# Moving the Fourier stage of a third batch into a feed-forward tail, loading normed rows a group ahead, and taking the first norms later

## The chip, the cores and the metric

The kernel runs on one core of a Trainium2 chip. The metric is the device time of one execution in microseconds (us), lower is better. The median of three executions of the kernel before is 1059.48 us. The core has a matrix engine (TensorE, PE), three engines for elementwise work (VectorE or DVE, ScalarE or ACT, GpSimd or POOL), and a queue engine (SyncE, SP) that here only issues transfers; ACT and POOL issue transfers too. Each engine works through its own list of instructions strictly in order.

## The reference, cut to what matters

Four batches of 576 rows and 512 columns (8 heads of 64 in the attention) go through three layers:

```python
x = attention(q, k, v)                 # thresholded softmax, 4 batches
k = np.maximum(xk @ w_k, 0.0)          # feed-forward block, xk and xr mix
v = k * k @ w_v                        # a row with the row before it
x = v / (1.0 + np.exp(-(xr @ w_r)))
u = x + real(fft(fft(x, axis=1), axis=2))     # Fourier stage, per batch
un = (u - mean(u)) / sqrt(var(u) + 1e-6)      # norm, per row
out = u + np.maximum(un @ w_ch1, 0.0) @ w_ch2 # channel mixer
```

Everything is float32. Products are made from high and low parts, three matmuls for one.

## The kernel before, in words

The rows of each batch are handled in two halves in the feed-forward block and in groups of 256 rows after it; there are nine groups, g = 0 to 8, two for each batch and one of remainder rows.

The **attention** fills the first half of the time, and the feed-forward blocks of the first batches run between its steps. The generator `ffn_stream` gives out the feed-forward work piece by piece: for each half a k phase (8 products `kps`), an r phase (4 products `rps`, whose gate is a tanh on ACT, L524) and a v phase (4 products `vps`, combined with the gate on DVE, L543); the rows are then transposed, copied to `xnat` by ACT (L572) and stored to DRAM (`xd[b]`, L574).

When the attention has ended, the loop `for _ in stream` (L1204) runs what is left of that generator: the v phase of the second half of batch 2, and all of batch 3. Beside each piece it advances other generators: `side`, the **Fourier stage** of batches 0 and 1, at 0.6 steps for each piece (`P['SR']`), with the norms of groups 0 and 1 between the steps of batch 1; and, from the middle of the last k phase on, `cgen`, which loads and unpacks the first quarter of the channel weights (`quarter(0)`, two pieces at a time). When the last r phase is done (`r_done`), groups 0 and 1 are transposed by `turn`.

The Fourier stage of a batch has 11 steps. `fft_fold` (6) loads the rows (`load_pairs`, and the remainder rows by `load_rem`) and folds them on DVE; `fft_one` (3) makes 35 matmuls (`f`); `fft_two` (2) makes 33 (`fz`, `fa`, `fb`), and `make_u` adds them on DVE into u and stores it (`ud[g]`, on SP).

The **channel mixer** (`mixer`, L1133) then goes through four quarters q of the weights and the nine groups in a written order that begins (0,0), (0,1), (0,2), (0,3), (1,0) to (1,3), (0,4). For each it makes `ch1` (`c1ps`, into two PSUM buffers, emptied by ACT L1119 and DVE L1120 into `hh`) and `ch2` (`c2ps`), adds the sum to `u` and stores that. Beside it the generator `behind` advances two steps for each piece: first `quarter(1)` (16 steps, each of four DVE passes over a tile `wraw` that ACT has issued a load for), then the Fourier stages of batches 2 and 3, then the remainder group and `done`, which frees the Fourier buffers. The norm of a later group is made at fixed places (`ahead_of`): group 2 in (0,0), group 3 in (0,1), and so on.

`norm(g)` loads the 256 rows of a group from `ud[g]` (two transfers, L995), takes statistics on DVE (L998), a square root on ACT (L1003), and scales the rows on ACT (L1011). Its rows live in a ring of four buffers with the tag "o", which `xnat`, the remainder rows of `load_rem` and `fft_last` use too.

The order in the source is a priority, not the final order: a planner places every instruction on its engine's list by its own estimate of when the inputs are there, and work of lower priority fills what it believes to be idle. Once placed, the order is fixed. The two lines of the source that speak of order most directly are these:

```python
    side = chain(fft_fold(0), fft_one(0), fft_two(0), fft_fold(1), norms(), fft_one(1), fft_two(1))
    ahead_of = {(0, 0): 2, (0, 1): 3, (1, 2): 4, (1, 3): 5, (0, 5): 6, (0, 6): 7, (0, 7): 8}
```

Of the kernel before, what the change touches and what calls it, by code (L numbers as in the profile page):

```python
# [10 lines left out]
F32 = mybir.dt.float32  # L11
# [9 lines left out]
D, FF, FC = 512, 1024, 2048  # L21
# [8 lines left out]
def tile_kernel(ctx: ExitStack, tc: tile.TileContext, a):  # L30
# [835 lines left out]
    def fft_fold(b):  # L866
        while written[b] < 2:
            yield
        settle()
        prs = prs_of[b] = load_pairs(b)  # L870
        ra, rb = load_rem(b)
        parts_e, parts_o = [], []
        for xa, xb in prs:
            e, o = folded(xa, xb, 128)
            yield
            parts_e.append(split_tile(e, 257, "fse"))
            parts_o.append(split_tile(o, 256, "fso"))
            yield
        e, o = folded(ra, rb, 98)
        yield  # L880
        ske = stack_tile(e, 257, "ske")
        sko = stack_tile(o, 256, "sko")
        fold_of[b] = (parts_e, parts_o, ske, sko)
        yield

    def fft_one(b):
        parts_e, parts_o, ske, sko = fold_of.pop(b)
        G = [fp.tile([128, 2, 290], F32R, tag=f"G{i}", bufs=1, name=f"G{i}") for i in range(2)]
        Hh = [fp.tile([128, 2, HS], F32R, tag=f"H{i}", bufs=1, name=f"H{i}") for i in range(2)]
        for mc in range(2):  # L890
            o = stage_1(parts_e, ske, tc1, tc1r, 290, 128 * mc, 128 * mc + 128)
            fsplit(G[0][:, mc], G[1][:, mc], o)
            o = stage_1(parts_o, sko, ts1, ts1r, HS, 128 * mc, 128 * mc + 128)
            fsplit(Hh[0][:, mc], Hh[1][:, mc], o)
            yield
        o = stage_1(parts_e, ske, tc1, tc1r, 290, 256, 257)
        fsplit(g1[0:1], g1[32:33], o)
        sl = slice(32 * b, 32 * b + 32)
        act.activation(g1[64:65, sl], o[:, 256:288], AF.Copy)
        dve.tensor_tensor(g1[96:97, sl], o[:, 256:288], g1[0:1, 256:288].bitcast(F32), op=ALU.subtract)  # L900
        for i, x in enumerate((G[0], G[1], Hh[0], Hh[1])):
            act.activation(grem[i][:, :, b, :], x[:, :, 256:288].bitcast(F32), AF.Copy)
        spec[b] = (G, Hh)
        yield

    def fft_two(b):
        G, Hh = spec.pop(b)
        prs = prs_of.pop(b)
        z, _ = stage_2(G, None, 0, 288, 289)
        zr = fp.tile([1, 257], F32, name="zr")  # L910
        act.activation(zr, z[0:1, 0:257], AF.Copy)
        for i in range(2):
            pa, pb = stage_2(G, Hh, 0, 128 * i, 128 * i + 128)
            make_u(2 * b + i, pa, pb, *prs[i], z=zr if i == 0 else None)
            yield

    def fft_last():
        xa = chp.tile([128, D], F32, tag="o", bufs=4, name="xar")
        xb = chp.tile([128, D], F32, tag="o", bufs=4, name="xbr")
        for b in range(B):  # L920
            sp.dma_start(xa[32 * b:32 * b + 32], xd[b][256:288, :])
            sp.dma_start(xb[32 * b:32 * b + 32], xd[b][544:576, :])
        gr = [x.rearrange("p c b r -> p c (b r)") for x in grem]
        pa, pb = stage_2(gr[0:2], gr[2:4], 64, 0, 128)
        make_u(8, pa, pb, xa, xb)
        yield

    def chain(*gens):
        for g in gens:
            yield from g  # L930
# [57 lines left out]

    uts, pairs, hs, more = {}, {}, {}, {}

    def norm(g):

        u = [chp.tile([128, D], F32, tag="o", bufs=4, name="un") for _ in range(2)]
        for j in range(2):
            sp.dma_start(u[j], ud[g][:, j])  # L995
        st = chp.tile([128, 32], F32, tag="lnst", bufs=1, name="lnst")
        for j in range(2):
            dve.bn_stats(st[:, 6 * j:6 * j + 6], u[j])  # L998
            dve.bn_aggr(st[:, 12 + 2 * j:14 + 2 * j], st[:, 6 * j:6 * j + 6])
        mean, var = st[:, 12:16:2], st[:, 13:16:2]  # L1000
        ve, sd, r0, t0, rstd, nb = (st[:, k:k + 2] for k in (16, 18, 20, 22, 24, 26))
        dve.tensor_scalar(ve, var, 1e-6, None, op0=ALU.add)
        act.activation(sd, ve, AF.Sqrt)  # L1003
        dve.reciprocal(r0, sd)
        dve.tensor_tensor(t0, r0, r0, op=ALU.mult)
        dve.tensor_tensor(t0, t0, ve, op=ALU.mult)
        dve.tensor_scalar(t0, t0, -0.5, 1.5, op0=ALU.mult, op1=ALU.add)
        dve.tensor_tensor(rstd, r0, t0, op=ALU.mult)
        dve.scalar_tensor_tensor(nb, mean, -1.0, rstd, op0=ALU.mult, op1=ALU.mult)
        for j in range(2):  # L1010
            act.activation(u[j], u[j], AF.Identity, scale=rstd[:, j:j + 1], bias=nb[:, j:j + 1])  # L1011
        return u
# [180 lines left out]
    fft_done, utp, ubp, hwp, xwp = False, None, None, None, None  # L1193
    normed = {}

    def norms():
        for g in range(2):
            normed[g] = norm(g)
            yield

    side = chain(fft_fold(0), fft_one(0), fft_two(0), fft_fold(1), norms(), fft_one(1), fft_two(1))
    cgen = None
    acc = 0.0
    for _ in stream:  # L1204
        for _ in range(2):
            if builds:
                builds.pop(0)()
        if len(pending) >= 2 or second:
            settle()
        acc += P['SR']  # L1210
        while acc >= 1:
            acc -= 1
            next(side, None)
        if ffn.get("r_done") and len(uts) < 2:
            g = len(uts)
            while g not in normed:
                next(side)
            turn(g, normed[g])
        if ffn.get("k_done") and cgen is None:
            cgen, pieces = quarter(0), 0  # L1220
        if cgen is not None:
            for _ in range(2):
                if pieces < 7 or ffn["k_done"] > 1:
                    next(cgen, None)
                    pieces += 1
# [7 lines left out]
    for _ in cgen:  # L1233
        pass
    behind = chain(
        quarter(1), fft_fold(2), fft_one(2), fft_two(2),
        fft_fold(3), fft_one(3), fft_two(3), fft_last(), done(),
    )

    ahead_of = {(0, 0): 2, (0, 1): 3, (1, 2): 4, (1, 3): 5, (0, 5): 6, (0, 6): 7, (0, 7): 8}  # L1240
# [1 line left out]
    for (q, gs), f in mixer():  # L1242
        g = gs[-1]
        credit += 2.0 if (q, g) < (0, 4) else 1.25 * len(gs)
        while credit >= 1:
            credit -= 1
            next(behind, None)
        if f == 2 and (q, g) in ahead_of:
            while (q, g) == (0, 5) and not fft_done:
                next(behind)  # L1250
            n = ahead_of[q, g]
            turn(n, norm(n))
        if (q, g) in ((1, 5), (2, 1)) and f == 3:
            for _ in behind:
                pass
            behind = quarter(q + 1)
        if q > 0 and g == 8 and f == 3:
            for _ in behind:
                pass
# [126 lines left out]
```

## Time and profile before

| | us |
|---|---|
| median of three executions | 1059.48 |
| lowest and highest | 1058.34, 1060.55 |
| the profiled execution, whole | 1057.07 |
| its span, first to last instruction | 1055.0 |
| PE busy within the span | 1004.3 |

The whole time of the profiled execution is 2.07 us more than its span. An engine's busy time leaves out its waits; of PE it has to be read with care, since matmuls overlap and their ends are modelled. The granted clock is the share of TensorE's full speed that the chip granted; its mean is 0.988.

### The profile page before, as it was taken

How to read it: one execution, taken by the hardware profiler on the slowest of the kernel's cores; microseconds unless marked ns; L12 is line 12 of the kernel's file. 1: busy time of each engine (PE TensorE's matmuls, PEld its weight loads, DVE VectorE, ACT ScalarE, POOL GpSimd, SP SyncE). 2: the span in 40 equal slices, each digit the busy share in tenths (PEclk: the TensorE clock that was granted, in tenths of full speed). 3: DMA queues.
4: the chain of work that ended last, by engine and by line, in shares of the span. 5: the costliest groups of instructions: out<-in, count | busy, mean ns of one | idle time of the engine just before them, and what ended most of it. 6: DMA issues, size and time to landing. Idle time of an engine off the chain costs nothing.

```text
span 1055.0 us, 18820 instructions
## 1 busy us (share of the span) xinstructions
PE 1004.3 (95%) x6807; PEld 884.6 (84%) x6807; DVE 715.9 (68%) x1880; ACT 536.6 (51%) x1211; POOL 395.8 (38%) x495
## 2 busy tenths in 40 slices
PE   5887889999999999999999988999999999999998
PEld 4565669988998888999799887898998888889997
DVE  6799988667776685865457978556537449236776
ACT  4688767675866757767265734342413113113332
POOL 1545868455574564843233101000014125112231
PEclk9899989999999999999999999999999999999999
DMA  6443331121211212100722656436325435223221
GB/s 223 149 134 86 112 108 60 48 72 38 72 60 54 66 47 72 51 24 14 209 72 88 205 186 200 157 103 226 129 89 184 130 114 179 97 99 122 101 100 61
DMA packets 45636, 114.52 MB, mean 109 GB/s; under 512 B 6319, under 2 KB 6740, under 8 KB 45544
## 3 DMA queue, kind: packets, MB, share of 16 engines
q1 hardware_dynamic: 27920, 74.47, 22.0%
q10 hardware_dynamic: 12344, 22.13, 6.8%
q0 software_dynamic: 5280, 16.72, 4.5%
q8 instruction: 54, 0.88, 0.4%
q14 instruction: 38, 0.31, 0.1%
HBM read 84.98 MB, written 28.32 MB: 107 GB/s over the span
## 4 chain that ended last, share of the span: by engine, by line
PE 73%; DVE 11%; DMA 7%; ACT 4%; issue 3%; POOL 1%; ACTq 0%; SPq 0%; DVEq 0%; POOLq 0%
PE c1ps L1109 6%; PE c1ps L1107 6%; PE c1ps L1108 6%; PE av L388 6%; PE s L227 5%; PE c2ps L1129 4%; PE c2ps L1131 4%; PE c2ps L1130 4%; PE p L1064 4%; PE t L329 4%; PE kps L408 2%; PE vps L536 2%; PE vps L537 2%; PE vps L538 2%; PE kps L409 2%
## 5 line engine op out<-in xcount | busy, mean ns | idle before, releaser
L267 DVE TENSOR_REDUCE small<-s 128x1 f32<-128x576 f32 x144 | 107.0, 752 | 48.1 <-PE s L227 36.9
L1178 POOL DMA_DIRECT2D ud<-u x54 | 29.4, 545 | 268.3 <-DVE u L1177 167.7
L290 POOL TENSOR_SCALAR e<-e,small 128x576 f32<-128x576 f32 x112 | 89.5, 806 | 89.0 <-DVE small L653 74.6
L282 DVE SCALAR_TENSOR_TENSOR e<-s,small,e 128x576 f32<-128x576 f32 x128 | 102.7, 812 | 25.4 <-ACT e L278 22.2
L278 ACT ACTIVATE e<-s,small 128x576 f32<-128x576 f32 x128 | 93.8, 744 | 29.4 <-DVE small L267 27.7
L1119 ACT ACTIVATE hh<-c1ps 128x256 fp32r<-128x256 f32 (+1 forms) x84 | 37.1, 443 | 138.4 <-PE c1ps L1109 114.7
L1120 DVE SCALAR_TENSOR_TENSOR hh<-c1ps,hh 128x256 fp32r<-128x256 f32 (+1 forms) x84 | 41.6, 497 | 86.6 <-ACT hh L1119 86.5
L329 PE MATMUL t<-ident,e 128*128 128x128 f32 x512 | 82.9, 279 | 10.2 <-ACT pt L332 4.6
L332 ACT ACTIVATE pt<-t 128x512 f32<-128x512 f32 x128 | 75.1, 599 | 22.8 <-PE t L329 21.0
L493 POOL TENSOR_TENSOR k<-relu,k 128x288 fp32r<-128x288 f32 x64 | 54.6, 855 | 68.4 <-ACT k L491 64.2
L329 PEld LDWEIGHTS t<-ident,e 128*128 128x128 f32 x512 | 61.6, 142 | 21.3 <-issue 6.5
L408 PE MATMUL kps<-xh,wk 128*128 128x288 f32 x256 | 78.2, 306 | 0.8 <-DVE fdd L851 0.3
L536 PE MATMUL vps<-k,wv 128*128 128x288 f32 x256 | 77.7, 305 | 0.4 <-ACT tg L524 0.4
L537 PE MATMUL vps<-k,wv 128*128 128x288 f32 x256 | 77.4, 303 | 0.0
L538 PE MATMUL vps<-k,wv 128*128 128x288 f32 x256 | 76.8, 301 | 0.0
L1107 PE MATMUL c1ps<-ut,cA 128*128 128x256 f32 (+1 forms) x224 | 71.2, 319 | 5.7 <-DVE hh L1120 4.0
L409 PE MATMUL kps<-xl,wk 128*128 128x288 f32 x256 | 76.3, 298 | 0.0
L410 PE MATMUL kps<-xh,wk 128*128 128x288 f32 x256 | 76.2, 298 | 0.0
L1109 PE MATMUL c1ps<-ut,cB 128*128 128x256 f32 (+1 forms) x256 | 76.0, 297 | 0.0
L1107 PE MATMUL c1ps<-ut,cB 128*128 128x256 f32 (+1 forms) x256 | 75.8, 296 | 0.0
L1108 PE MATMUL c1ps<-ut,cB 128*128 128x256 f32 (+1 forms) x256 | 75.7, 296 | 0.0
L1108 PE MATMUL c1ps<-ut,cA 128*128 128x256 f32 (+1 forms) x224 | 70.8, 316 | 0.2 <-DVE ut L1028 0.2
(273 smaller groups left out, 3117.4 us busy)
## 6 DMA issues: line engine op xcount, KB each, us to landing
u<-ud SPq DMA_DIRECT2D x36, 512.0 KB
wraw<-in_w_ch ACTq DMA_DIRECT2D x64, 256.0 KB
rawqk<-in_qk SPq DMA_DIRECT2D x24, 608.0 KB
ud<-u POOLq DMA_DIRECT2D x54, 256.0 KB, 2.6
v<-in_v SPq DMA_DIRECT2D x16, 320.0 KB
un<-ud SPq DMA_DIRECT2D x18, 256.0 KB
out<-u SPq DMA_DIRECT2D x18, 256.0 KB
wraw<-in_w_k SPq DMA_DIRECT2D x8, 512.0 KB
```

Of the source, the lines that this page charges most:

```text
L267: dve.tensor_reduce(st[:, 0:1], sps[n][:, :, 0:HS], axis=AX.XY, op=ALU.max, negate=True)
L278: act.activation(two(eview(n)), sps[n][:, :, 0:HS], AF.Exp, bias=st[:, 0:1])
L282: dve.scalar_tensor_tensor(e, sps[n][:, :, 0:HS], st[:, 1:2], e, op0=ALU.is_ge, op1=ALU.mult, accum_out=st[:, 2:3])
L329: pe.transpose(t[:, k, :], e[:, o + 128 * k:o + 128 * (k + 1)], ident)
L408: pe.matmul(ps, wh, x[0][k], start=(k == 0), stop=False)
L409: pe.matmul(ps, wh, x[1][k], start=False, stop=False)
L536: pe.matmul(ps, wv[0][:, c:c + 128], k2[0][:, k, :], start=(k == 0), stop=False)
L537: pe.matmul(ps, wv[0][:, c:c + 128], k2[1][:, k, :], start=False, stop=False)
L538: pe.matmul(ps, wv[1][:, c:c + 128], k2[0][:, k, :], start=False, stop=(k == 7))
L1107: pe.matmul(ps, wh, ut[0][:, k, :], start=(k == 0), stop=False)
L1108: pe.matmul(ps, wh, ut[1][:, k, :], start=False, stop=False)
L1109: pe.matmul(ps, wl, ut[0][:, k, :], start=False, stop=(k == 3))
```

## The change

Three things change. `norm` takes its rows from a list `fetched`, and a new function `fetch` issues the two loads; for group 2 that is done right after the `turn` of group 1, for groups 3, 7 and 8 right after the `turn` of the group before. The generator `side` advances one whole step for each piece and has no norms in it; when it is used up, the loop goes on with a new generator `third`, the Fourier stage of batch 2, of which `behind` takes only what is left. The norms of groups 0 and 1 are made one each at the first two pieces after the last k phase, instead of between the steps of batch 1.

```diff
+    fetched = {}
+
+    def fetch(g):
+        fetched[g] = [chp.tile([128, D], F32, tag="o", bufs=4, name="un") for _ in range(2)]
+        for j in range(2):
+            sp.dma_start(fetched[g][j], ud[g][:, j])
+
     def norm(g):
 
-        u = [chp.tile([128, D], F32, tag="o", bufs=4, name="un") for _ in range(2)]
-        for j in range(2):
-            sp.dma_start(u[j], ud[g][:, j])
+        if g not in fetched:
+            fetch(g)
+        u = fetched.pop(g)
...
-    def norms():
-        for g in range(2):
-            normed[g] = norm(g)
-            yield
-
-    side = chain(fft_fold(0), fft_one(0), fft_two(0), fft_fold(1), norms(), fft_one(1), fft_two(1))
+    side = chain(fft_fold(0), fft_one(0), fft_two(0), fft_fold(1), fft_one(1), fft_two(1))
+    third = chain(fft_fold(2), fft_one(2), fft_two(2))
     cgen = None
-    acc = 0.0
     for _ in stream:
...
-        acc += P['SR']
-        while acc >= 1:
-            acc -= 1
-            next(side, None)
+        if ffn.get("k_done", 0) > 1 and len(normed) < 2:
+            for _ in side:
+                pass
+            normed[len(normed)] = norm(len(normed))
+        elif next(side, 1):
+            next(third, None)
         if ffn.get("r_done") and len(uts) < 2:
             g = len(uts)
-            while g not in normed:
-                next(side)
             turn(g, normed[g])
+            if g == 1:
+                fetch(2)
...
     behind = chain(
-        quarter(1), fft_fold(2), fft_one(2), fft_two(2),
-        fft_fold(3), fft_one(3), fft_two(3), fft_last(), done(),
+        quarter(1), third, fft_fold(3), fft_one(3), fft_two(3), fft_last(), done(),
     )
...
             turn(n, norm(n))
+            if n in (2, 6, 7):
+                fetch(n + 1)
```

## Rows read from the trace of the kernel before

**Rows 1.** The page: busy time of each engine, share of the span, instructions.

```profile
PE 1004.3 (95%) x6807; PEld 884.6 (84%) x6807; DVE 715.9 (68%) x1880; ACT 536.6 (51%) x1211; POOL 395.8 (38%) x495
```

**Rows 2.** Busy time by stretch: length, engines (instructions), granted clock, DMA share, GB/s.

```profile
505.00:560.00 55.00, 52.38 (x380) 48.11 (x379) 28.95 (x69) 24.09 (x73) 18.74 (x29) 1.00 0.53 159
560.00:599.00 39.00, 37.21 (x273) 34.79 (x271) 34.21 (x105) 29.45 (x76) 11.12 (x11) 1.00 0.36 113
599.00:620.00 21.00, 20.97 (x159) 20.65 (x160) 18.35 (x53) 10.13 (x27) 0.00 (x0) 1.00 0.56 164
620.00:640.00 20.00, 16.16 (x94) 14.44 (x93) 14.53 (x48) 7.45 (x17) 1.18 (x2) 0.91 0.70 235
640.00:660.00 20.00, 16.50 (x101) 13.80 (x99) 16.75 (x54) 8.58 (x22) 2.24 (x4) 1.00 0.69 212
660.00:700.00 40.00, 40.00 (x274) 36.52 (x275) 24.84 (x73) 13.91 (x43) 1.62 (x3) 1.00 0.41 139
700.00:780.00 80.00, 80.00 (x534) 71.89 (x533) 41.10 (x117) 26.92 (x62) 5.92 (x11) 1.00 0.42 145
```

**Rows 3.** The same view, the two stretches after those of the change.

```profile
780.00:960.00 180.00, 180.00 (x879) 150.54 (x877) 89.77 (x175) 37.19 (x80) 48.65 (x72) 1.00 0.41 133
960.00:1055.00 95.00, 90.55 (x755) 89.62 (x753) 70.49 (x148) 30.33 (x49) 23.87 (x19) 1.00 0.25 90
```

**Rows 4.** Waits of PE, 599 to 660 us: total, times, longest.

```profile
PE c1ps L1107 <- DVE hh L1120: 4.0, 2, 3.8
PE c1ps L1107 <- ACT ut L1027: 1.6, 1, 1.6
PE c2ps L1129 <- ACT hh L1119: 1.3, 1, 1.3
```

**Rows 5.** Timeline of PE, 620 to 632 us: start, duration, idle before.

```profile
624.71 0.58 PE L1107 MATMUL c1ps<-ut,cA 128*128 128x256 f32 x1 [3.84 <-DVE hh L1120]
...
627.43 0.73 PE L1131 MATMUL c2ps<-cA,hh 128*128 128x512 f32 x2
...
628.91 0.28 PE L1107 MATMUL c1ps<-ut,cA 128*128 128x256 f32 x1
...
630.34 0.63 PE L1131 MATMUL c2ps<-cA,hh 128*128 128x512 f32 x2
```

**Rows 6.** Timeline of DVE, 618 to 647 us.

```profile
618.37 0.43 DVE L71 SCALAR_TENSOR_TENSOR wbits<-wraw,wbits 128x256 int32<-128x256 int32 x1
623.30 0.69 DVE L998 BATCH_NORM_STATS2 lnst<-un 128x6 f32<-128x512 f32 x1 [4.50 <-DMA un<-ud]
...
624.23 0.42 DVE L1120 SCALAR_TENSOR_TENSOR hh<-c1ps,hh 128x256 fp32r<-128x256 f32 x1
...
646.10 0.29 DVE L69 TENSOR_SCALAR wbits<-wraw 128x256 int32<-128x256 int32 x1 [2.65 <-DMA wraw<-in_w_ch]
```

**Rows 7.** The chain that ended last, 616 to 646 us: start, duration, what.

```profile
616.54 6.74 DMA un<-ud
...
639.15 6.85 DMA wraw<-in_w_ch
```

**Rows 8.** Waits of PE, 560 to 599 us.

```profile
PE rps L408 <- ACT relu L478: 0.9, 1, 0.9
```

**Rows 9.** Instructions on the tile un, 555 to 660 us: duration ns min/median/max, first and last.

```profile
L998 DVE BATCH_NORM_STATS2 lnst<-un x8: 675/688/695, 573.3 to 640.2; 128x6 f32<-128x512 f32 x8
L1011 ACT ACTIVATE un<-un,lnst x8: 799/802/817, 582.7 to 655.5; 128x512 f32<-128x512 f32 x8
```

**Rows 10.** Waits of SP's transfer queue, 505 to 700 us.

```profile
SPq L995 <- DMA xd<-xnat: 13.2, 4, 6.9
```

**Rows 11.** Timeline of ACT, 592 to 602 us.

```profile
592.88 1.28 ACT L524 ACT_TABLE_LOAD   x1
594.18 0.41 ACT L524 ACTIVATE tg<-rps 128x288 f32<-128x288 f32 x1
...
601.10 0.21 ACT L792 ACTIVATE fp<-xa 128x2 f32<-128x2 f32 x1 [0.55 <-DMA xa<-xd]
```

## The prediction

> **What bounds the kernel now.** I read the page first. PE is busy for 1004.3 us, 95% of the span [rows 1], and the change removes no matmul. So it can only win back time in which PE waits, or runs at a lower clock; the next view is therefore busy time by stretch, around the places that the diff touches. PE's idle time is the length of a stretch less its busy time [rows 2]: 2.62 us in 505 to 560, 1.79 in 560 to 599, 0.03 in 599 to 620, 3.84 in 620 to 640, 3.50 in 640 to 660, and none from 660 to 780. That is 11.8 us in all, and it is all that the three edits can aim at; from 780 to 960 PE is busy throughout, and the 4.45 us idle at the end [rows 3] lie in the last quarter, which the edits don't touch. The attention ahead of 505 us isn't touched either.
>
> Then I asked what ended the largest idle times. In 620 to 640 it is one wait of 3.84 us for DVE's `hh` [rows 4, 5]. DVE wasn't busy then: it finished an unpacking pass at 618.80 and stood 4.50 us at the statistics of group 2 until their rows landed, and the `hh` that PE wanted lay behind them on its list [rows 6]. The chain shows the transfer: issued at 616.54, 6.74 us until it landed [rows 7], while the core moved 235 GB/s [rows 2]. After the wait the granted clock is down (mean 0.91 over the stretch [rows 2]): the 12 `c1ps` matmuls from 624.71 took 2.72 us until 627.43, the 12 from 628.91 took 1.43 us [rows 5], so 1.29 us went at the lower of the two levels, 1.2 GHz, after an idle time of 3.84 us. In 640 to 660 two waits stand out [rows 4]: 1.6 us for the transposed rows of group 3 (ACT `ut`), and 1.3 us for ACT's `hh` at about 647.7, which comes right after DVE stood 2.65 us at a weight tile `wraw` [rows 6] that took 6.85 us to land [rows 7].
>
> **The change part by part**, against the profiled execution's 1057.07 us.
>
> *Group 2 fetched ahead.* Its loads are issued when `turn` of group 1 has been placed, and wait only for a buffer that `turn` of group 0 frees; in the trace of before that would be some 10 us ahead of 616.54. The transfer of 6.74 us [rows 7] is then over before the statistics come up. That removes 3.84 us of idle time and 1.29 us of low clock: **-5.1 us**. Bounds: -5.1, and 0 if another wait ends as late.
>
> *Group 3 fetched ahead* removes its load from the stretch 640 to 660, where DVE is busy for 16.75 of 20 us [rows 2]. The 1.6 us wait for `ut` belongs to group 3, so I take it as gone; the 1.3 us wait hangs on a weight tile, which isn't fetched any earlier, so I leave it. **-1.6 us**, bounds 0 and -3.5 (the whole idle time). Groups 7 and 8: 0, since PE is never idle there [rows 3].
>
> *The Fourier stage of batch 2 moves forward.* By the code it is 35 + 33 = 68 matmuls; at the pace of 599 to 620 us (159 in 21 us, 0.132 us each [rows 2]) that is 9.0 us of PE. With it go some 37 DVE passes of about 0.42 us (the price of `hh` [rows 6]), 15 us; some 27 ACT copies; and 18 transfers on SP (4 loads and 4 stores of 256 KB, 10 loads of remainder rows), which now stand ahead of the loads of groups 0 and 1 in SP's queue. It leaves a stretch where PE wasn't idle (660 to 700 [rows 2]) and so gives back exactly its own 9.0 us; it enters the stretch 520 to 610, where it costs 9.0 us and what waits it brings. In steps: `side` now ends after 22 pieces and `third` after 33, and by my count of the generator the last k phase ends at about piece 38, so the stage is through before the norms start. DVE has room: 63.2 busy of 94 us from 505 to 599, 78.7 of 103 with the 15.5 added. The cover for its cost is thus PE's own feed-forward matmuls, which need no DVE until they end. The nearest row for its waits is batch 1, which sat in 560 to 599 with 1.79 us of idle time [rows 2], half of it (0.9) a wait for a `relu` behind other work on ACT [rows 8]. I take the other half, **+0.9 us**; bounds -1.8 (the idle time there is filled by the new matmuls) and +2.6 (as dear as 505 to 560, where the tables arrive).
>
> *The quicker pace of batches 0 and 1* moves work within a stretch in which DVE is idle nearly half the time (28.95 of 55 us [rows 2]): 0. If the cover goes, the bounds of the edit above hold for it too.
>
> *Norms of groups 0 and 1 later.* Each is two loads, two statistics passes of 0.69 us on DVE and two scalings of 0.80 us on ACT [rows 9]. They leave the last k phase, where PE waited 0.9 us for a `relu` behind them on ACT [rows 8]; Fourier work of batch 2 takes their place there, so I take nothing back for it. They enter the r phase, some 48 matmuls (6.3 us at the pace above) before the v phase in which they are transposed. There they meet the tanh of the gate on ACT, and the r phase has two PSUM buffers that only the tanh empties: what is queued behind a square root that waits is a tanh, and PE waits for that. Square root and tanh use different tables: the trace of before shows a load of 1.28 us just ahead of a tanh [rows 11]. If the planner places a root between two tanh there are two more loads, 2.57 us. I take half of these as uncovered: **+1.3 us**. Bounds: -0.9 (the wait for `relu` goes and nothing comes), and +10.2: each of the two loads of rows uncovered as that of group 2 was, 2 x 3.84 us [rows 5], and 2.57 us of tables.
>
> The Trainium skill ("ScalarE: Activation LUTs", What ACT_TABLE_LOAD costs) puts a switch at about 2.66 us, a load of 1283 ns and a drain of about 1380 ns, and says to do all functions of one set before the next; this speaks against this edit. The trace agrees on the load, 1.28 us, and the tanh starts 0.02 us after its end [rows 11]; it shows no drain there. By the page's figure the two loads would cost 5.3 us instead of 2.57, and the sum below would be 1.4 us higher.
>
> *Buffers.* Four buffers "o" are shared. Group 2's rows now hold two of them when the last three `xnat` are due, so the third `xnat` waits until the store of the first has landed. Before, the loads of L995 waited for such stores, 13.2 us in four waits, the longest 6.9 [rows 10]; that wait had no one behind it on SP, while `xnat` sits on ACT with `hh` behind it. The planner knows the buffer and can put `hh` first: 0, bound +3.84.
>
> Sum: -5.1 - 1.6 + 0.9 + 1.3 = **-4.5 us**: 1052.6 for the profiled execution, which lies 2.41 us below the median. Against the median that is 1059.48 - 4.5 = **1055.0 us**. A measurement of this kernel can tell about 0.2%, 2.1 us, from no change.
>
> **The rivals.**
>
> *The wait moves to the third `xnat` (0.17).* The buffer wait above comes out at its bound: PE stands at `c1ps` as long as before, only for another transfer. For: the row of 6.9 us, and 235 GB/s at that place. Against: the first store is issued before `hh` is due. The time: the -5.1 falls away, +0.6 us, 1060.1. No change.
>
> *The wait moves to the first norms (0.13), slower.* Their loads are now the only ones not fetched ahead, and are issued in a phase in which the weights of quarter 0 are loaded. If both come as late as group 2's did, DVE and ACT stand in the r phase, PE twice for 3.84 us, and the tables are switched twice more: 10.2 us, against 6.7 gained and 0.9 for the stage: +4.4, 1063.9. It decides once the r phase loses more than 5.8 us. For: the same loads on the same queue, ACT busy for 29.45 of 39 us in 560 to 599, and DVE for 18.35 of 21 in the stretch after [rows 2]. Against: DMA is busy for 0.36 and 0.56 there, not 0.70, and SP can issue a load as soon as a buffer is free. The table rule cited above is the smaller half of this case.
>
> *More of the idle time goes (0.20).* The matmuls of batch 2 fill PE where it waits in the k phase, and DVE, 15 us lighter after 640 us, is on time in the mixer: -5.1 - 3.5 - 1.8 + 1.3 = -9.1, 1050.4. Against: `quarter(1)` and the fold of batch 3 take the place of batch 2 there.
>
> *Nothing comes of it (0.05)*: the planner had already begun the fold of batch 2 at 601 us [rows 11], so its order changes little: 1059.5.
>
> **How the numbers follow.** Forecast 0.45, its own range 1052.5 to 1057.4. Faster: forecast and the third rival, 0.65. Same: the first and the last, 0.22. Slower: 0.13. The range reaches down past the third rival, almost to the sum of all lower bounds (-5.1 - 3.5 - 1.8 - 0.9 = -11.3, 1048.2), and up past the first (1060.1); it leaves out the slower one: 1048.5 to 1060.8.
>
> **What would show it.** Right: DVE has no wait over 1 us for `un` of group 2, and PE none over 1 us at `c1ps` between the first `c1ps` and 20 us later; no low clock there; the first `c1ps` comes about 9 us later than before, with 68 more Fourier matmuls ahead of it. Wrong: PE idle for more than 3 us in the last r phase, with ACT's tanh or the root as releaser, or ACT standing at `xnat` after the last v phase, or three or more table loads around that r phase.

## The result and the profile after

| | before | after |
|---|---|---|
| median (6 executions each, beside one another) | 1058.87 us | 1065.86 us |
| lowest and highest | 1055.9 to 1060.55 | 1063.21 to 1067.02 |
| ratio, 95% interval | | 1.0068 [1.0049, 1.0086] |
| profiled execution: span | 1055.0 us | 1063.8 us |

The kernel became 7 us slower where 4.5 us faster was forecast. The direction was wrong, and the time lies above the range. In two of the experiments below one execution took far longer than the others (1982 us and 1243 us); it is left out of their medians and ratios. In the code after, lines behind L995 stand seven further down (`c1ps` is L1114, `hh` L1126 and L1127, the loads of a norm L996, the transposes of `turn` L1031), and in some experiments one further still.

Busy time by stretch, kernel after, columns as in [rows 2]:

```profile
505.00:560.00 55.00, 52.59 (x382) 47.88 (x379) 28.29 (x68) 24.19 (x73) 18.75 (x29) 1.00 0.55 162
560.00:599.00 39.00, 38.87 (x289) 37.03 (x288) 31.60 (x91) 26.76 (x70) 10.77 (x11) 1.00 0.34 104
599.00:620.00 21.00, 17.38 (x112) 15.24 (x111) 18.33 (x63) 9.08 (x25) 0.00 (x0) 0.90 0.64 204
620.00:640.00 20.00, 15.38 (x83) 12.62 (x83) 18.36 (x61) 12.43 (x30) 0.00 (x0) 0.76 0.62 194
640.00:660.00 20.00, 16.63 (x107) 14.08 (x105) 15.04 (x50) 9.18 (x27) 0.00 (x0) 1.00 0.67 196
660.00:700.00 40.00, 39.75 (x269) 35.88 (x269) 27.25 (x86) 15.60 (x41) 3.51 (x6) 1.00 0.53 178
```

The loss sits in one place. Up to 599 us the kernel after is a little ahead (16 more matmuls in 560 to 599 than [rows 2], and the wait for `relu` of [rows 8] is gone). From 599 to 660 PE makes 302 matmuls where before it made 354 [rows 2]. That shows the place and not the size, since matmuls differ in length and a few per cent of the records can be missing. The size can be estimated from the rows. From 560 to 660 us PE idles for 11.7 us (9.2 before). The granted clock falls to 0.90 and 0.76 of full speed in two of the stretches, which is up to 6.9 us (0.10 of 21 and 0.24 of 20); before it was up to 1.8 (0.09 of 20). Together that is 7.7 us more than before. It is an upper estimate, as a lower clock costs nothing while PE stands.

What PE did meanwhile, timeline of PE after, 612 to 637 us:

```profile
612.30 0.30 PE L538 MATMUL vps<-k,wv 128*128 128x288 f32 x1
...
615.22 0.55 PE L451 MATMUL xl<-ident,tg 128*128 128x128 f32 x3 [1.32 <-DVE tg L543]
...
619.51 0.45 PE L819 MATMUL f<-tc,fseh 128*128 128x290 f32 x1
619.75 0.44 PE L820 MATMUL f<-tc,fsel 128*128 128x290 f32 x1
...
629.27 0.38 PE L836 MATMUL fa<-talt,g 33*128 33x258 f32 x1
630.05 0.63 PE L1031 MATMUL ut<-ident,un 128*128 128x128 f32 x4 [0.40 <-DVE fdd L853]
632.05 0.63 PE L1031 MATMUL ut<-ident,un 128*128 128x128 f32 x4 [1.38 <-DVE fdd L853]
633.37 0.80 PE L1114 MATMUL c1ps<-ut,cA 128*128 128x256 f32 x2 [0.69 <-ACT ut L1034]
...
636.30 1.12 PE L1031 MATMUL ut<-ident,un 128*128 128x128 f32 x4 [1.28 <-DVE ut L1035]
```

The last matmul of the v phase starts at 612.30 us. Then PE has little but the Fourier matmuls of batch 2, and it waits again and again for a copy or a subtraction of the step before. The last, a `fa`, starts at 629.27, and only behind it come the transposes of group 0 and, at 633.37, the first `c1ps`. From the last `vps` to the first `c1ps` pass 21.1 us. Before, they were 0.38 us apart, with three transposes between them:

```profile
613.33 0.30 PE L538 MATMUL vps<-k,wv 128*128 128x288 f32 x1
...
613.71 0.36 PE L1107 MATMUL c1ps<-ut,cA 128*128 128x256 f32 x1
```

In the kernel after, the matmuls at 619.5 come 0.24 us apart, those around 612 and earlier 0.13: the lower of the two clock levels, after a stretch in which PE waited again and again.

Why the stage came so late, SP's queue after:

```profile
541.43 0.25 SPq L786 DMA_DIRECT2D rb<-xd  x1
...
595.62 0.32 SPq L862 DMA_DIRECT2D ud<-xb  x1
598.08 0.80 SPq L773 DMA_DIRECT2D xa<-xd  x2
...
612.60 0.80 SPq L996 DMA_DIRECT2D un<-ud  x2
...
630.70 0.32 SPq L996 DMA_DIRECT2D un<-ud  x1
```

and ACT's timeline after:

```profile
596.71 1.28 ACT L1010 ACT_TABLE_LOAD   x1
598.00 0.20 ACT L1010 ACTIVATE lnst<-lnst 128x2 f32<-128x2 f32 x1
598.22 1.28 ACT L524 ACT_TABLE_LOAD   x1
599.52 0.41 ACT L524 ACTIVATE tg<-rps 128x288 f32<-128x288 f32 x1
602.53 0.21 ACT L792 ACTIVATE fp<-xa 128x2 f32<-128x2 f32 x1 [2.29 <-DMA xa<-xd]
603.05 1.52 ACT L1018 ACTIVATE un<-un,lnst 128x512 f32<-128x512 f32 x2
...
640.55 0.59 ACT L572 ACTIVATE xnat<-xl 32x512 f32<-32x512 f32 x1 [1.71 <-DMA xd<-xnat]
...
642.34 0.38 ACT L1126 ACTIVATE hh<-c1ps 128x256 fp32r<-128x256 f32 x1 [1.21 <-issue]
```

The rows of batch 2 go into the tiles `xa` and `xb` of batch 1, which are free only when batch 1's u is stored. Those stores are issued up to 595.62, the load follows at 598.08, and the first fold of batch 2 starts at 602.53: 1.4 us later than before, where it started at 601.10 [rows 11]. So in time the fold wasn't moved at all. What moved is the rest of the stage, from beside the mixer to ahead of it. The loads of the remainder rows were issued by 541.43; these rows lie in two of the four buffers "o" for some 70 us until they are folded, and the rows of group 1 get a buffer only at 612.60. The rows fetched "ahead" for group 2 are issued at 630.70, 14 us later than before [rows 7].

### The profile page after: what moved, and what is told of

Read it like the earlier page. It is cut to its first block, busy times and chain, and to the rows that moved or that the text cites. A ratio compares the mean times of both kernels' runs of the same rounds, so it can differ in the third digit from the quotient of the medians.

```text
span 1063.8 us, 18838 instructions
## 1 busy us (share of the span) xinstructions
PE 1005.9 (95%) x6807; PEld 885.1 (83%) x6807; DVE 715.9 (67%) x1880; ACT 536.7 (50%) x1211; POOL 395.5 (37%) x495
## 4 chain that ended last, share of the span: by engine, by line
PE 70%; DVE 12%; DMA 8%; issue 4%; ACT 3%; POOL 2%; ACTq 0%; SPq 0%; DVEq 0%; POOLq 0%
PE c1ps L1114 6%; PE c1ps L1116 6%; PE c1ps L1115 6%; PE av L388 5%; PE s L227 5%; PE c2ps L1138 5%; PE c2ps L1136 4%; PE c2ps L1137 4%; PE p L1071 4%; PE t L329 3%; PE kps L408 2%; DMA rawqk<-in_qk 2%; PE kps L409 2%; PE kps L410 2%; DVE small L267 2%
## 5 line engine op out<-in xcount | busy, mean ns | idle before, releaser
L1126 ACT ACTIVATE hh<-c1ps 128x256 fp32r<-128x256 f32 (+1 forms) x84 | 37.1, 443 | 152.5 <-PE c1ps L1116 126.0
L1127 DVE SCALAR_TENSOR_TENSOR hh<-c1ps,hh 128x256 fp32r<-128x256 f32 (+1 forms) x84 | 41.5, 495 | 104.8 <-ACT hh L1126 103.3
L1114 PE MATMUL c1ps<-ut,cB 128*128 128x256 f32 (+1 forms) x256 | 76.1, 297 | 0.0
L1114 PE MATMUL c1ps<-ut,cA 128*128 128x256 f32 (+1 forms) x224 | 70.8, 318 | 1.4 <-ACT ut L1034 0.7
```

The source lines that it names most:

```text
L1114: pe.matmul(ps, wh, ut[0][:, k, :], start=(k == 0), stop=False)
```

## The experiments

Theory **A**: the stage of batch 2 is a chain of dependent steps that outlasts the feed-forward block and stands ahead of the transposes of groups 0 and 1. **B**: the late norms cost the time. **C**: the fetched rows hold the buffers "o". Later theories about what makes the chain dear: **S**, it starts too late, since its rows wait for `xa` and `xb`; **D**, DVE's list is full from 580 to 660 us; **P**, the transposes are kept behind the chain by their place in the order or for want of a PSUM buffer; **R**, the remainder rows hold buffers "o" that group 1 needs. "Own before" is the kernel before, run beside each kernel; its median lay between 1057.83 and 1059.22 us, so a difference between two kernels that weren't run beside one another is good to some 1.4 us.

### The parts taken apart

Only fetching, on the kernel before (`fetch` as in the change, called in the same places):

```diff
+            if g == 1:
+                fetch(2)
...
+            if n in (2, 6, 7):
+                fetch(n + 1)
```

> The kernel before with the fetching ahead alone (groups 2, 3, 7, 8). Theory A (the Fourier stage of batch 2, moved forward, is a serial chain that outlasts the feed-forward block and keeps PE waiting): 1053 to 1056 us, the 3.8 us wait of PE at c1ps is gone and nothing takes its place. Theory B (the late norms of groups 0 and 1 are what costs): the same 1053 to 1056. Theory C (the fetched rows hold two of the four buffers o that the last xnat need): 1059 to 1063, with ACT waiting at xnat.

All of the change but batch 2, which stays in the mixer:

```diff
-        elif next(side, 1):
-            next(third, None)
+        else:
+            next(side, None)
```

> The kernel after with batch 2 left to the mixer: fetching ahead, one step for each piece, late norms. Theory A: 1053 to 1057, 9 to 13 us faster than after, the first c1ps is back at about 614 us. Theory B: 1063 to 1067, as slow as after. Theory C: about 1060 to 1064, between the two.

The same without fetching (pace and late norms alone), and the kernel after without fetching; both leave out the two calls of `fetch` shown above:

> The same without the fetching: one step for each piece and late norms alone. Theory A: 1057 to 1061, within 2 us of before, and with its 3.8 us wait. Theory B: 1064 to 1070, slower by what the first norms cost. Theory C: 1057 to 1061.

> The kernel after without the fetching: batch 2 moved forward, one step for each piece, late norms. Theory A: 1066 to 1071, so that fetching is worth 0 to 5 us in after too. Theory B: the same. Theory C: 1058 to 1062, faster than after, with no ACT wait at xnat.

And, later, the kernel before with the quicker pace alone:

```diff
-        acc += P['SR']
-        while acc >= 1:
-            acc -= 1
-            next(side, None)
+        next(side, None)
```

> The kernel before with the quicker pace alone (one step of the Fourier generators at each piece instead of 0.6; norms stay ahead of batch 1's second half). Pace and late norms together gave -5.0 us. If the pace gives it: 1053 to 1055.5. If the later norms give it: 1058 to 1061, as before. The prediction had put the pace at 0 and the late norms at +1.3.

| kernel | us | own before | ratio, 95% interval |
|---|---|---|---|
| fetching alone | 1054.41 | 1059.22 | 0.9946 [0.9927, 0.9966] |
| pace + late norms | 1054.25 | 1059.22 | 0.9952 [0.9932, 0.9971] |
| pace alone | 1053.39 | 1057.83 | 0.9954 [0.9937, 0.9970] |
| fetching + pace + late norms | 1049.67 | 1059.22 | 0.9900 [0.9879, 0.9921] |
| after without fetching | 1064.72 | 1059.22 | 1.0044 [1.0032, 1.0057] |
| after | 1065.86 | 1058.87 | 1.0068 [1.0049, 1.0086] |

B and C fall. Everything but batch 2 is worth -9.6 us, the sum of fetching (-4.8) and of pace with late norms (-5.0). The two kernels with the pace and the late norms came out faster than any theory expected of them, since none had a gain from the pace. The pace alone gives -4.4, so the late norms cost nothing that can be measured here. Moving batch 2 costs 16.2 us (1065.86 - 1049.67). Without fetching it costs 10.5 (1064.72 - 1054.25): 5.7 us of the 16.2 are the gain of fetching, which in the kernel after is worth nothing.

The kernel without the move shows why. Busy time by stretch and PE's timeline, fetching + pace + late norms:

```profile
560.00:599.00 39.00, 38.76 (x288) 36.93 (x288) 30.70 (x88) 26.50 (x72) 11.46 (x13) 1.00 0.38 118
599.00:620.00 21.00, 19.54 (x152) 18.88 (x152) 19.22 (x66) 12.20 (x28) 0.00 (x0) 1.00 0.64 198
620.00:640.00 20.00, 19.26 (x124) 17.16 (x123) 18.28 (x61) 10.03 (x25) 1.18 (x2) 1.00 0.73 230
640.00:660.00 20.00, 20.00 (x138) 18.61 (x138) 17.00 (x51) 10.51 (x27) 1.34 (x3) 1.00 0.69 204
```

```profile
603.90 0.60 PE L1031 MATMUL ut<-ident,un 128*128 128x128 f32 x4
...
611.69 0.29 PE L538 MATMUL vps<-k,wv 128*128 128x288 f32 x1
...
613.20 0.36 PE L1114 MATMUL c1ps<-ut,cA 128*128 128x256 f32 x1
```

Group 0 is transposed at 603.90, inside the v phase, and the mixer starts 1.5 us after the last `vps`; the 414 matmuls of the three stretches from 599 stand against 302 after. From 560 to 660 us PE idles for 2.4 us, 9.3 less than after, and the clock stays at 1.00, against the up to 6.9 us above: by this estimate the two make up the 16.2. DVE is as full as in the kernel after (19.22 of 21, 18.28 of 20 us) and PE doesn't mind, because it has matmuls that don't wait for it. The rows of batch 2 load neither earlier nor later in it, at 598.44.

Where the pace found its gain, waits of PE from 600 to 660 us with the pace alone:

```profile
PE c1ps L1107 <- DVE hh L1120: 2.0, 1, 2.0
PE c1ps L1108 <- DVE ut L1028: 0.7, 1, 0.7
```

The 3.8 us of [rows 4] are 2.0, the 1.6 for `ut` are 0.7, and the 1.3 for ACT's `hh` are gone. Batch 1 ended sooner in this run: the rows of batch 2 load at 587.95 instead of 597.02. But that can't be what carries the gain, since with pace and late norms they load at 596.84 and the gain is the same. By what way the quicker pace helps is open.

It does bear on the move. The pace by itself frees `xa` 9 us sooner, and with the late norms that is gone: in the kernel after the load comes at 598.08. The move with the quicker pace and the norms in their old place was not run; the next section shows what early rows are worth there.

### When the chain starts, and the transposes behind it

Batch 2's main rows taken from a table in SBUF as a stand-in, so that the fold waits for no store and no load; then its remainder rows alone, which then hold no buffer "o"; then both:

```diff
-        for xa, xb in prs:
+        flat = tc1.bitcast(F32).rearrange("p a b c -> p (a b c)")
+        for xa, xb in [(flat[:, 0:512], flat[:, 512:1024])] * 2 if b == 2 else prs:
```

```diff
-        ra, rb = load_rem(b)
+        rows = tc1.bitcast(F32).rearrange("p a b c -> p (a b c)")
+        ra, rb = (rows[:98, 0:512], rows[:98, 512:1024]) if b == 2 else load_rem(b)
```

> The kernel after, but the main rows of batch 2 are folded from a table that lies in SBUF already (its values stand in for them), so that the fold needn't wait until batch 1 has given back the two buffers for its rows. Theory S (the chain of batch 2 starts too late for that block, because its rows wait for those buffers): 1050 to 1057, the Fourier matmuls of batch 2 lie under the last v phase or ahead of it. Theory D (DVE has too much to do from 600 to 640 us, whenever batch 2 starts): 1058 to 1063. Theory P (PE's order: the transposes of groups 0 and 1 are placed behind the chain of batch 2): 1060 to 1066 if they stay behind it.

> The kernel after, but the remainder rows of batch 2 come from that table, so that they never hold two of the four buffers o. Theory R (those buffers, held from about 530 to 614 us, keep the rows of group 1 and the last xnat waiting): 1055 to 1061. Theories S, D and P: 1063 to 1067.

> The kernel after, with both the main rows and the remainder rows of batch 2's fold read from a table in SBUF (wrong values): the fold waits for no stores and no loads, and holds no buffer of the rows to be normed. The early main rows alone gave -6.4 us, the free buffers alone nothing here (but -6.6 where only the fold was moved). If these two things together are the 16 us: 1049 to 1053. If the two further steps of batch 2, 33 matmuls with their copies ahead of the first c1ps, cost by themselves: 1056 to 1060, as with the early rows alone.

With early main rows the kernel takes 1059.42 us, ratio 1.0015 [1.0000, 1.0030]. That is above the 1050 to 1057 that S expected, and inside the range of D. With the stand-in for the remainder rows alone it takes 1067.47, 1.0083 [1.0058, 1.0108] (three executions), so there is no gain. With both it takes 1058.16, 1.0008 [0.9995, 1.0021], which is no more than the main rows alone give. So the late start (S) is worth 6.4 us of the 16 by the medians, 5.6 by the ratios; R is worth nothing in the full change. PE's timeline with early main rows:

```profile
613.37 0.30 PE L538 MATMUL vps<-k,wv 128*128 128x288 f32 x1
...
622.26 0.38 PE L836 MATMUL fa<-talt,g 33*128 33x258 f32 x1
622.57 0.66 PE L1032 MATMUL ut<-ident,un 128*128 128x128 f32 x4
...
627.14 0.80 PE L1115 MATMUL c1ps<-ut,cA 128*128 128x256 f32 x2 [0.21 <-ACT ut L1035]
```

The fold now begins at 588.42 and its first matmul is at 600.22 (602.53 and 607.83 after). The chain ends 7 us earlier and still outlasts the v phase by 9 us; the first `c1ps` comes 13.8 us after the last `vps`, not 21.1. So even with early rows the stage isn't through before the norms start, which the prediction had counted on.

The transposes put ahead in the order (a priority of 4000 steps for the four `pe.transpose` of `turn`), and, separately, the transposes of groups 0 and 1 in a PSUM buffer that the stage's `f` and `fa` don't use, though its `fb` does:

```diff
+            with tc.high_priority(offset=4000):
```

```diff
-            t = pst.tile([128, 4, 128], F32, tag="t", name="ut")
+            t = (psx if g < 2 else pst).tile([128, 4, 128], F32, tag="fa" if g < 2 else "t", name="ut")
```

> The kernel after, with the transposes of the normed rows placed as early as the planner believes them ready (a higher priority). Theory P: 1052 to 1059. Theories S and D: 1062 to 1067, since the Fourier matmuls still stand ahead of most of the mixer with nothing beside them.

> The kernel after, with the transposes of groups 0 and 1 put into the PSUM buffer fa instead of one of the two buffers t that the Fourier matmuls of batch 2 hold. Theory P (the turn of group 0 is placed behind batch 2 for want of a buffer, and the mixer with it, so that PE has nothing to run beside the chain): 1050 to 1057, the transposes of group 0 at about 605 to 612 us and the first c1ps well ahead of 633. Theory D (DVE has too much to do there): 1060 to 1066. Theory S (the chain starts too late) alone: 1062 to 1067.

They take 1064.95 and 1063.86 us, 1.0066 [1.0043, 1.0088] and 1.0059 [1.0041, 1.0076]. The first transposes with the priority, and then, in the other buffer, with ACT's copy ahead of them:

```profile
628.40 0.63 PE L1032 MATMUL ut<-ident,un 128*128 128x128 f32 x4 [0.40 <-DVE fdd L853]
```

```profile
627.12 0.36 ACT L850 ACTIVATE fdd<-fb 128x256 f32<-128x256 f32 x1
```

```profile
627.61 0.66 PE L1031 MATMUL ut<-ident,un 128*128 128x128 f32 x4
```

The transposes stayed right behind the last `fa` (627.62 and 627.29), so neither run tests what an early transpose would give. The traces point at the PSUM buffers. In the kernel after and with the priority, the first transpose waits for the `fdd` of DVE that empties a `fa`, which holds one of the two buffers that `f`, `fa` and `ut` share. In the other run it starts once ACT's `fdd` has emptied the second `fb`, which holds the only buffer of that kind. So both times the transposes needed a buffer that the stage used to its end. A run that gives them one that is free wasn't made, so the cause is argued and not shown.

### How full DVE is

The pass over the weights' low parts of quarters 0 and 1 on POOL instead of DVE; then one of the four DVE passes over their pieces left out (the second line of the second diff alone), 11 us of DVE's work (704.5 us instead of 715.9); then two of the four, 21 us (DVE is busy for 695.0 us instead of 715.9), on the kernel after and on the kernel with batch 2 in the mixer:

```diff
-            yield from weight_pieces(todo, None, stage2, 256, rb=3, bb=2, lows=dve if q < 2 else None)
+            yield from weight_pieces(todo, None, stage2, 256, rb=3, bb=2, lows=None)
```

```diff
-            dve.scalar_tensor_tensor(w, h, -0x40000000, w, op0=ALU.bitwise_and, op1=ALU.bitwise_or)
-            dve.scalar_tensor_tensor(w, l, 29, w, op0=ALU.logical_shift_right, op1=ALU.bitwise_or)
+            if lows is None:
+                dve.scalar_tensor_tensor(w, h, -0x40000000, w, op0=ALU.bitwise_and, op1=ALU.bitwise_or)
+                dve.scalar_tensor_tensor(w, l, 29, w, op0=ALU.logical_shift_right, op1=ALU.bitwise_or)
```

> The kernel after, with one of the four DVE passes for each weight piece of quarters 0 and 1 given to POOL, which is idle there: about 13 us of DVE time fewer from 575 to 670. Theory D: 1056 to 1062. Theories S and P: 1063 to 1067.

> The kernel after with one of the four DVE passes on each of the 32 weight pieces of quarters 0 and 1 left out (the one that fills the low bits): 10.7 us of DVE less, nothing put in its place. Theory D: 1055 to 1061. Theories P and S: 1062 to 1067.

> The kernel after, with two of the four DVE passes over each weight piece of quarters 0 and 1 left out (the low bits of those weights are then wrong): 64 passes, some 21 us less on DVE's list, with batch 2 still moved forward. Theory D (the 16 us are DVE work for which the list is full from 580 to 660 us): 1050 to 1053, within 4 us of x2. Theory A (the 16 us are the latency of the chain of batch 2, which ends after the v phase and stands ahead of the turns on PE, whatever DVE has besides): 1061 to 1064, some 11 us or more above x2.

> The same lighter weight pieces on the kernel with batch 2 left in the mixer (rows fetched ahead, quicker pace, norms late): the partner of x1. It had no wait over 2 us left, so both theories expect 1046 to 1050 here. What decides is x1 less x2: 0 to 4 us by theory D, 11 us or more by theory A; between 5 and 10 each has a part.

With the pass on POOL the kernel takes 1064.04 us (1.0056 [1.0037, 1.0075]). That run says nothing about D, because DVE was no freer: it was busy for 716.9 us, against 715.9, as its other passes took longer (L71 487 ns in the mean from 560 to 680 us, against 415). With one pass left out it takes 1063.80 (1.0045 [1.0023, 1.0066]), in the range of P and S and not of D. With two it takes 1064.78 (1.0057 [1.0038, 1.0075]), and the partner 1053.97 (0.9948 [0.9928, 0.9968]). The difference of the pair is 10.8 us: near the 11 that A expected, far from the 0 to 4 of D. Busy time by stretch with the light pieces on the kernel after, and three lines of PE's timeline:

```profile
600.00:620.00 20.00, 19.21 (x120) 18.84 (x119) 12.96 (x43) 10.42 (x27) 0.00 (x0) 0.79 0.53 176
620.00:640.00 20.00, 15.11 (x91) 12.14 (x91) 16.26 (x52) 12.31 (x34) 0.00 (x0) 0.81 0.69 228
```

```profile
598.98 0.61 PE L409 MATMUL rps<-xr,wr 128*128 128x288 f32 x1 [2.73 <-ACT tg L525]
...
620.75 0.30 PE L539 MATMUL vps<-k,wv 128*128 128x288 f32 x1
...
635.60 0.80 PE L1115 MATMUL c1ps<-ut,cA 128*128 128x256 f32 x2 [0.69 <-ACT ut L1035]
```

DVE has 7.0 and 3.7 of 20 us free, and the first `c1ps` comes no earlier (635.60; after: 633.37). The gap behind the last `vps` did shrink, from 21.1 to 14.9 us, but the v phase ended 8 us later. That is a limit of this pair, and the trace shows where it comes from: the planner's order is another when DVE is lighter, and in the r phase PE stands 2.73 us for a tanh and then works at the lower clock (0.79 from 600 to 620). That tanh stands on ACT behind a copy of a weight piece, which waits for DVE, which stands 2.69 us for the rows of group 0. This is the wait at the late norms that theory B meant, and it is not in the kernel after. The partner waits for a tanh too, 1.98 us behind the two table loads of a root, and became 4.3 us slower than it was with the full work. So the sizes are good to some 4 us; that is enough to say that a full DVE isn't the main part.

### Which step brings it

The whole stage behind the loop, first in the mixer; only the fold in the loop; the fold and the first step (as the second diff, with `fft_one(2)` in `third`):

```diff
-        quarter(1), third, fft_fold(3), fft_one(3), fft_two(3), fft_last(), done(),
+        third, quarter(1), fft_fold(3), fft_one(3), fft_two(3), fft_last(), done(),
```

```diff
-    third = chain(fft_fold(2), fft_one(2), fft_two(2))
+    third = fft_fold(2)
...
-        quarter(1), third, fft_fold(3), fft_one(3), fft_two(3), fft_last(), done(),
+        quarter(1), third, fft_one(2), fft_two(2), fft_fold(3), fft_one(3), fft_two(3), fft_last(), done(),
```

> The kernel after, with batch 2 out of the loop but ahead of quarter 1 in the mixer's side work, so that groups 0 and 1 are turned before it and the mixer's matmuls may run beside it. Theory P: 1048 to 1054, near the kernel without the third batch (1049.7). Theory D: 1055 to 1064, since DVE has the same work in the same 60 us. Theory S: 1048 to 1054.

> The kernel after, with only the fold of batch 2 in the loop (loads and DVE work), its matmuls and make_u behind quarter 1. Theory P: 1048 to 1055, since no Fourier matmul of batch 2 stands ahead of the turn. Theories D and S: 1055 to 1062, as the fold is half of the DVE work and begins as late as before.

> The kernel after, with the fold and the first step of batch 2 in the loop and only its second step behind quarter 1. The fold alone gave 1057.3, all three 1065.9. If the 8.6 us between them are spread over the steps by their matmuls and copies: 1060 to 1063. If they belong to the second step, the last of the chain ahead of the turns: 1056.5 to 1058.5. If the first step alone brings them: 1064 to 1067.

They take 1056.64 us (0.9990 [0.9968, 1.0012]), 1057.31 (0.9990 [0.9971, 1.0009]) and 1059.65 (1.0010 [0.9997, 1.0022]). With the stage in its old place, behind quarter 1, the kernel takes 1049.67. Against that, its place first in the mixer costs 7.0 us; in the loop, the fold costs 7.6, the first step 2.3 more, the second 6.2 more, each to some 1.4 us.

The first of these runs came out in the range of D and above that of P. Here nothing of batch 2 stands ahead of the transposes of groups 0 and 1, and the loss comes later: from 640 to 700 us PE idles for 4.5 us, where it idled for none with the stage behind quarter 1, and the granted clock is 0.91. Of these 4.5 us, 1.1 is the transposes of a later group waiting for an `fdd` again, and 1.4 are waits inside the stage (`fa`, `fb`, `fz`). So an early stage costs something there too, and A as it is put doesn't cover that. The last run fell just below the 1060 to 1063 of an even spread. In its trace 27 `f` and, pulled ahead by the planner, 12 `fb` stand between the v phase and the mixer, and the first `c1ps` comes 17.7 us after the last `vps`. The full second step adds 21 more matmuls, and the two `fdd` of its `make_u` that the transposes waited for.

Why the fold alone costs 7.6 us, with the remainder rows as a stand-in in this kernel too:

> Only the fold of batch 2 is in the loop, its other steps behind quarter 1, and the remainder rows of batch 2 are read from a table in SBUF instead of from loaded rows (wrong values), so that they hold no buffer of the rows to be normed. Theory R (those buffers keep the rows of group 1 back, and the turn of group 1 waits 5 us for them): 1050 to 1053, against 1057.3 with the loaded rows. Theory D or A: 1056 to 1058, no different.

It takes 1050.75 us, 0.9917 [0.9890, 0.9943]: 6.6 of the 7.6 us are back. Here R holds. Waits of PE from 600 to 660 us, fold alone, then with the stand-in:

```profile
PE ut L1031 <- ACT un L1018: 5.1, 1, 5.1
PE xl L451 <- DVE tg L543: 1.7, 1, 1.7
```

```profile
PE xl L451 <- DVE tg L543: 2.4, 3, 1.1
PE c2ps L1137 <- ACT xnat L572: 0.6, 1, 0.6
```

and the statistics of group 1 on DVE, in the same order:

```profile
610.16 0.69 DVE L1005 BATCH_NORM_STATS2 lnst<-un 128x6 f32<-128x512 f32 x1
611.42 0.69 DVE L1005 BATCH_NORM_STATS2 lnst<-un 128x6 f32<-128x512 f32 x1
```

```profile
605.98 1.28 DVE L1006 BATCH_NORM_STATS2 lnst<-un 128x6 f32<-128x512 f32 x2
```

With the buffers held, the statistics of group 1 are 4 to 5 us late, its scaled rows with them, and PE waits 5.1 us for the rows to transpose. The full change hides this: there PE is still in the chain at 622 us, and the scaled rows of group 1 (627.66 us) aren't last. The same held buffers are worth 6.6 us in one kernel and nothing in the other.

## Why the prediction was wrong

The failed step is the cost of the moved stage, put at +0.9 us with bounds of -1.8 and +2.6, and measured at +16.2 us. It rested on one sentence: "`side` now ends after 22 pieces and `third` after 33 ... so the stage is through before the norms start". That sentence counts generator steps, which give the order in the source, and takes them for the time at which the work can run. The row that speaks against it was in the document: batch 2's fold began at 601.10 before, in a wait for `xa` that had just ended [rows 11]. The load into `xa` has to wait for batch 1's last stores, which the change as a whole left where they were, and the fold began at 602.53.

With that, the cover that the prediction counted on is gone. The feed-forward matmuls end at 612.30, so 60 of the stage's 68 matmuls run with hardly anything beside them. At 0.132 us each they are 7.9 us, which are given back later, as the prediction said. What isn't given back is the waiting and the low clock. Most of it falls into the gap behind the v phase: 21.1 us less the 7.9, and less the 1.5 of the gap without the move, are 11.7. The other 4.5 of the 16.2 us must come elsewhere; behind the first `c1ps` the trace shows the turn of group 1 in single file with its copies (1.28 us at 636.30), and a wait of 1.70 at `hh`. And the transposes of group 0, whose rows were ready at 604.6, stand behind the chain.

Shown by the runs: the move costs 16.2 us; early rows take off some 6 of them; moving the steps one at a time costs 7.6, 2.3 and 6.2; 21 us less work on DVE takes off some 5, give or take 4. Not settled: whether the PSUM buffers alone keep the transposes behind the last `fa`, and how the 9.8 us that remain with early rows divide between DVE's list, the latency of each step and the place of the transposes.

The other terms:

- *Fetching*, -6.7 (-5.1 and -1.6): -4.8 alone, interval -3.6 to -7.7 by the ratio. This term was right in mechanism, and its size lies within the interval. The wait of 3.84 us at `c1ps` [rows 5] is 1.3 us in the kernel that only fetches, and the clock there stays at 1.00. In the kernel after fetching gives nothing; there the loads for group 2 come at 630.70, behind the chain.
- *The quicker pace*, 0: -4.4. The prediction looked only at the stretch in which the work was done. PE waits less later, in the mixer; why is open, as said above.
- *Late norms*, +1.3, bounds -0.9 and +10.2: nothing measurable where they were measured, with batch 2 in the mixer (pace with late norms -5.0, pace alone -4.4). In the kernel after they undo the earlier end of batch 1 that the pace alone gives; what that costs was not run. The rows above show a root between two tanh with its two table loads, at 596.71 and 598.22, of 1.28 us each; PE had no wait of theirs listed from 560 to 600. The Trainium skill ("ScalarE: Activation LUTs", What ACT_TABLE_LOAD costs) gives a drain of some 1380 ns on top of the load; here, as in [rows 11], each load starts within 0.02 us of the end of the activation before it, and the next activation 0.01 or 0.02 us after the load, so that no drain is seen.
- *Buffers "o"*, 0, bound +3.84: the third `xnat` did wait, 1.71 us at 640.55, and an `hh` behind it, and behind transfers that ACT issued in between, held PE for 1.70 us. So this rival came about, at under half its price, and with it one of the prediction's own signs of being wrong. The larger harm of these buffers, the remainder rows of batch 2 in front of group 1's norm, wasn't named.
- *The slower rival* (1063.9) came near the time by the wrong mechanism: the r phase lost nothing, PE having only 0.13 us idle in 560 to 599. That the time fits is luck. The rival that the change does nothing saw that the fold of batch 2 had begun at 601 us and drew "its order changes little" from it; what it should have drawn is that the stage comes too late for its cover.

The best kernel of the study leaves batch 2 in the mixer and keeps the rest: 1049.67 us, 0.9900 [0.9879, 0.9921] of before.

## What to carry to other kernels

When a chain of dependent steps is moved forward, look first for the row that shows when its first input can be there (a store that must land, a tile that must come free), and lay its length against the end of the work that is to cover it; a count of generator steps says nothing of either. In a list whose order is fixed ahead, what starts late delays all that stands behind it, ready or not, so ask what the next stage's first instruction will stand behind. And an early load into a shared ring takes its buffer from whoever asks next: the worth of the same buffer was 6.6 us or none, by which wait ended last.

Before a run counts as a test, read from its trace that its edit did what it was for: with the pass on POOL, DVE was as busy as before, and the other PSUM buffer was one that the stage held too.

## What was not expected of the hardware

PE's waits in the chain were short, mostly 0.2 to 1.4 us each, and still the granted clock fell to 0.90 and 0.76 over two stretches of some 20 us, where before a stretch with one wait of 3.84 us had 0.91 [rows 2]. The matmuls from 619.5 us came 0.24 us apart at the lower level, those at 623 again 0.13.
